# Output tiles and small copies on ScalarE, no identity turns ahead of a read, another order of the work, in a fused attention and FFN kernel

## The chip, the cores and the metric

The kernel runs on one core of a Trainium2 chip. Its engines have queues of their own, each worked off in order: TensorE (PE for its matmuls, PEld for its weight loads), VectorE (DVE), ScalarE (ACT), GpSimd (POOL) and SyncE (SP), which issues most of the DMAs. The metric is the time of one execution on the device in microseconds, the median of several runs.

## The reference

```python
# x (8, 8, 512, 64): B, H, S, D;  state (8, 8, 32, 64): B, H, Ns, D
scores = scale * x @ state^T;   a  = softmax(scores)   # over the 32 states
xread  = a @ state                                     # (B, H, 512, 64)
scores2 = scale * state @ x^T;  a2 = softmax(scores2)  # over the 512 tokens
sread  = a2 @ x                                        # (B, H, 32, 64)
x_in = concatenate([xread, sread], axis=2)             # 544 tokens of a batch
x_in = x_in.transpose(0, 2, 1, 3).reshape(8 * 544, 512)
h = x_in @ w_in                  # w_in (512, 2048)
g = h * clip(h + 3, 0, 6) / 6
out = g @ w_out                  # w_out (2048, 512); out (4352, 512)
```

All inputs and the output are float32.

## The kernel before

A float32 product is made of three matmuls: both factors are split into a high part, rounded to the matmul's format (fp32r), and a low part, the rest; hi x hi, hi x lo and lo x hi add up in one bank (`product`, L1053). ScalarE makes the high parts (L402, and L524 for w_out), VectorE the low ones (L403, L526). Weights come as 16-bit halves that are put together on chip (L492 on ScalarE, L497 on VectorE).

The FFN runs in two sweeps over the hidden dimension. A sweep has a unit for each batch b (512 tokens, four tiles of 128), and a small unit for all state tokens; a unit has eight steps, one for each 128 hidden columns. In a step TensorE forms a hidden tile in a `ps_h` bank (L1053; in the opening's first steps one plain float32 matmul for each part, L1274); ScalarE takes relu(h + 3) into `g` (L1295), VectorE min(., 6) times h (L1298), both split g into `g_hi` and `g_lo`, and TensorE multiplies it with the step's rows of w_out into four accumulators `acc0` to `acc3`, one for each tile of tokens (L1053, plain ones L1355). The attention is folded into that: the scores' softmax weights are multiplied with state times w_in (`wp_hi`, `wp_lo`, made from L630) instead of with the state first. At a unit's end in the first sweep the accumulators, times 1/6, go to an output tile `ot` in `put_out`: tiles with an even number by ScalarE (L1380), the others by VectorE (L1383), and from there to the partial result. The second sweep (from about 320 us) goes over the other half of the hidden columns and works with sums of quarters (L1165).

The second softmax is made beside the first sweep. For b = 0 its weights are turned by TensorE (L940) and copied by ScalarE (L944); `tokens_read_alone` then lets TensorE read the tokens (L1008), for b = 0 behind eleven identity turns (L1034). The result, divided and turned, goes to `sread_t` through `put` (L985, eight copies of 128x128). Identity turns of another kind (L1660) stand in the opening wherever the plan leaves TensorE a gap.

No loop sets the order of the instructions. Every operation is put on a list by `plan.add` with an engine, an estimated cost, what it reads and writes, and `Plan.order` schedules it: each engine takes, of the operations that can start within 0.3 us of the earliest, the one with the lowest number in RANKS (L24 to L133, a number for each operation). `issue` emits the instructions in that order, and each engine's queue keeps it. So the table decides what stands behind what on an engine; buffers and banks are given out in that order too.

The names in the rows: `raw`, `early` are staging tiles of weights or of x, `tops` high halves of weights, `tmp` tiles of 128x512, `st_raw` the state, `a0hi` and `a0lo` copies of the split weights of b = 0 that are stored in memory for the second sweep (L1424). L617 loads 64 KB of x for the transposes L720, which make the x that the scores L630 of the next batch need; four tiles of 128x512 are one batch, four loads make one, eight stand in one buffer `raw`.

Of the kernel before, what the change touches and what calls it, by code (L numbers as in the profile page):

```python
# [279 lines left out]
def tile_state_attention_then_hardswish_ffn(  # L280
# [8 lines left out]
    nc = tc.nc  # L289
    B, H, S, D = x.shape  # L290
# [693 lines left out]
    def put(c, ps, cols):  # L984
        V(0.28, URGENT, lambda: nc.vector.tensor_copy(  # L985
            sread_t.rearrange("p q (n b) -> p q n b", b=B)[..., c],
            bank(ps)[:, cols].rearrange("p (q n) -> p q n", n=NS)), [ps], [("sread", c)],
            [scores_at[0]])
# [702 lines left out]
```

## Time and profile before

| what | value |
|---|---|
| median of 3 runs | 638.37 us (637.26 to 639.91) |
| the profiled execution | 639.32 us, its span 637.5 us |
| TensorE matmuls | 630.1 us busy, 4388 instructions |
| VectorE | 520.4 us (82%), 946 instructions |
| ScalarE | 343.9 us (54%), 611 instructions |
| granted TensorE clock | 1.00 |

The span is what the profiler sees between the first and the last instruction; 1.82 us of the execution lie around it. Matmuls are pipelined, so that the durations of their records overlap: in a run of products one of 128x512 starts every 0.23 us, while its record says 0.39. An idle time in square brackets behind a row is the time that the engine stood idle before it, and what ended that.

### The profile page before, as it was taken

The numbers are of one execution on the slowest core, as the hardware profiler recorded it, in microseconds if no ns is written. First come the engines' busy times: TensorE is split into PE (matmuls) and PEld (weight loads), VectorE is DVE, ScalarE is ACT, GpSimd is POOL, SyncE is SP. The second block draws the span as 40 slices with busy tenths as digits, with TensorE's granted clock in tenths as the row PEclk, the third lists the DMA queues.
The fourth block names the chain that finished last, engine by engine and source line by source line (L and its number), as shares of the span: only waits on it lengthen the run. The fifth ranks groups of instructions, "written<-read, shape, count | busy, mean of one in ns | idle before, by whom it ended". The sixth has DMA issues, their size and how long they took to land.

```text
span 637.5 us, 11454 instructions
## 1 busy us (share of the span) xinstructions
PE 630.1 (99%) x4388; PEld 528.3 (83%) x4388; DVE 520.4 (82%) x946; ACT 343.9 (54%) x611; POOL 18.4 (3%) x22
## 2 busy tenths in 40 slices
PE   8999999999999999999999999999999999999997
PEld 7467778777777778778888888899999999999996
DVE  5999998988988797885568738999979899988773
ACT  4865565545555554454446657665455455554431
POOL 0000000000000000000000000000000000001010
PEclk9999999999999999999999999999999999999999
DMA  8987995967687695540312868324626225522244
GB/s 293 268 224 122 260 175 142 213 153 207 110 208 176 149 219 117 141 99 9 93 67 87 293 209 228 110 38 97 133 34 166 34 34 125 107 34 34 34 67 99
DMA packets 168261, 86.18 MB, mean 135 GB/s; under 512 B 128528, under 2 KB 152976, under 8 KB 168080
## 3 DMA queue, kind: packets, MB, share of 16 engines
q1 hardware_dynamic: 164240, 77.47, 46.9%
q0 software_dynamic: 3824, 7.87, 8.6%
q8 instruction: 34, 0.56, 0.4%
q14 instruction: 19, 0.16, 0.1%
q10 hardware_dynamic: 144, 0.13, 0.1%
HBM read 50.84 MB, written 34.60 MB: 134 GB/s over the span
## 4 chain that ended last, share of the span: by engine, by line
PE 92%; SPq 2%; DMA 2%; DVE 1%; ACT 1%; issue 0%
PE acc L1053 31%; PE acc L1165 24%; PE ps_h L1053 23%; PE ps_s L1053 7%; PE ps_s L630 2%; SPq L617 2%; DMA st_raw<-in_state_dram 2%; PE ps_s L1491 1%; PE ps_h L1008 1%; PE acc L1491 1%; PE ps_h L630 1%; PE acc L1355 1%; DMA raw<-in_x_dram 0%; PE acc L730 0%; PE ps_s L794 0%
## 5 line engine op out<-in xcount | busy, mean ns | idle before, releaser
L1053 PE MATMUL acc<-w_out_hi,g_hi 128*128 128x512 f32 x296 | 118.2, 399 | 0.3 <-ACT g_hi L402 0.3
L1053 PE MATMUL acc<-w_out_lo,g_hi 128*128 128x512 f32 x296 | 115.5, 390 | 0.0
L1053 PE MATMUL acc<-w_out_hi,g_lo 128*128 128x512 f32 x296 | 115.4, 390 | 0.0
L1165 PE MATMUL acc<-w_out_hi,tmp 128*128 128x256 f32 x360 | 87.9, 283 | 0.0
L1295 ACT ACTIVATE g<-ps_h,three 128x512 f32<-128x512 f32 (+1 forms) x80 | 51.2, 646 | 57.9 <-PE ps_h L1053 52.3
L1298 DVE SCALAR_TENSOR_TENSOR g<-g,ps_h 128x512 f32<-128x512 f32 (+1 forms) x80 | 50.1, 629 | 27.6 <-ACT g L1295 27.0
L1053 PEld LDWEIGHTS acc<-w_out_hi,g_hi 128*128 128x128 f32 x296 | 55.6, 188 | 19.4 <-issue 7.0
L1165 PE MATMUL acc<-w_out_hi,g_lo 128*128 128x256 f32 x240 | 68.0, 283 | 0.0
L1165 PE MATMUL acc<-w_out_lo,g_hi 128*128 128x256 f32 x240 | 67.9, 283 | 0.0
L1165 PE MATMUL acc<-w_out_hi,g_hi 128*128 128x256 f32 x240 | 67.9, 283 | 0.0
L1053 PE MATMUL ps_h<-aT_hi,wp_hi 128*128 128x512 f32 (+1 forms) x188 | 67.6, 360 | 0.0
L1165 PEld LDWEIGHTS acc<-w_out_hi,tmp 128*128 128x128 f32 x360 | 66.4, 192 | 0.3
L1053 PE MATMUL ps_h<-aT_lo,wp_hi 128*128 128x512 f32 (+1 forms) x188 | 66.5, 354 | 0.0
L1053 PE MATMUL ps_h<-aT_hi,wp_lo 128*128 128x512 f32 (+1 forms) x188 | 66.4, 353 | 0.0
L1053 PEld LDWEIGHTS acc<-w_out_hi,g_lo 128*128 128x128 f32 x296 | 55.6, 188 | 12.3 <-DVE g_lo L403 0.4
L1053 PEld LDWEIGHTS acc<-w_out_lo,g_hi 128*128 128x128 f32 x296 | 55.6, 188 | 10.7 <-issue 0.3
L402 ACT CAST g_hi<-G 128x512 fp32r<-128x512 f32 (+1 forms) x64 | 38.2, 606 | 46.8 <-PE acc L1165 38.7
L402 ACT CAST g_hi<-g 128x512 fp32r<-128x512 f32 (+1 forms) x74 | 42.7, 585 | 27.3 <-DVE g L1298 16.6
L403 DVE TENSOR_TENSOR g_lo<-g,g_hi 128x512 fp32r<-128x512 f32 (+1 forms) x74 | 46.8, 643 | 8.7 <-ACT g_hi L402 6.6
L1165 PE MATMUL acc<-w_out_lo,tmp 128*128 128x256 f32 x180 | 50.9, 283 | 0.0
L403 DVE TENSOR_TENSOR g_lo<-G,g_hi 128x512 fp32r<-128x512 f32 (+1 forms) x64 | 42.2, 669 | 6.1 <-ACT g_hi L402 5.5
L1165 PEld LDWEIGHTS acc<-w_out_hi,g_hi 128*128 128x128 f32 x240 | 46.0, 192 | 0.7
(179 smaller groups left out, 1277.5 us busy)
## 6 DMA issues: line engine op xcount, KB each, us to landing
out_dram<-ot SPq DMA_DIRECT2D x8, 1024.0 KB, 5.3
W<-G SPq DMA_DIRECT2D x16, 512.0 KB, 4.1
out_dram<-ot POOLq DMA_DIRECT2D x15, 512.0 KB, 6.0
raw<-in_x_dram SPq DMA_DIRECT2D x112, 64.0 KB, 2.9
xb<-in_x_dram SPq DMA_DIRECT2D x28, 256.0 KB, 4.7
raw<-in_moe_w_out_dram SPq DMA_DIRECT2D x11, 511.8 KB, 5.1
wp_lo<-W SPq DMA_DIRECT2D x40, 128.0 KB, 2.8
raw<-in_moe_w_in_dram SPq DMA_DIRECT2D x8, 511.0 KB, 5.5
```

The source lines that it names most:

```text
L402: first = S_(cost, rank, lambda: nc.scalar.copy(hi(), src()), reads, [writes[0]], after)
L403: V(cost, rank, lambda: nc.vector.tensor_tensor(lo(), src(), hi().bitcast(F32), op=ALU.subtract), [*reads, writes[0]], [writes[1]])
L617: nc.sync.dma_start(t[rows, i].rearrange("t (a c) -> t a c", c=NS), x[b, 4 * g + 2 * i + u, :, k * NS : (k + 1) * NS].rearrange("(a t) c - ...
L630: nc.tensor.matmul(out[u][cols, :], made["stT", b][rows, cols], moving(q)[rows], start=True, stop=True,)
L1008: nc.tensor.matmul(bank(pr)[cols, u * D : (u + 1) * D], e2T(b, u)[:, j * P + q * NS : j * P + (q + 1) * NS], x_tile(b, True)[:, NG * q + u ...
L1053: nc.tensor.matmul(ps, l, r, start=start and k == 0, stop=stop and k == n - 1)
L1165: nc.tensor.matmul(out, left(a, l), right(b, r), start=p == 0 and z == 0 and y == 0, stop=p == FPS // 2 - 1 and y == 2, skip_group_check=True)
L1295: in_turn["g", n] = S_(cost + 0.05, rank, lambda: nc.scalar.activation(g(), bank(ps)[:, :width], AF.Relu, bias=three, scale=-1.0 if turned ...
L1298: V(cost, rank, lambda: nc.vector.scalar_tensor_tensor(g(), g(), 6.0, bank(ps)[:, :width], op0=ALU.min, op1=ALU.mult), [ps], [g_key])
L1355: nc.tensor.matmul(bank(acc), made["g_hi", n][:, js], plain_out[f][1](), start=opens, stop=closes)
L1491: nc.tensor.matmul(bank(banks[q // 2][u])[:, q % 2 * W : (q % 2 + 1) * W], st[l]()[rows, q], wp(r)[rows, q], start=y == 0, stop=y == 2, sk ...
```

## The change

Four things: `put` copies on ScalarE instead of VectorE; the eleven identity turns of `tokens_read_alone` are gone (and the operation's estimated cost goes from + 0.2 to + 0.25); in `put_out` all four output tiles of a unit of the first sweep (b < B) go to ScalarE; and RANKS has other numbers. The lines behind L1034 are numbered two lower in the new kernel (L1295 is L1293, L1298 is L1296, L1380 is L1378).

```diff
 RANKS = [int(k) for k in """
-2 0 8 3 33 1 18 4 38 20 28 11 21 37 40 25 31 53 58 29 36 39 43 57
+2 0 7 3 27 1 11 4 31 13 24 10 14 30 33 23 26 43 47 25 28 32 34 46
...
     def put(c, ps, cols):
-        V(0.28, URGENT, lambda: nc.vector.tensor_copy(
+        S_(0.28, URGENT, lambda: nc.scalar.copy(
             sread_t.rearrange("p q (n b) -> p q n b", b=B)[..., c],
...
         def run():
-            for _ in range(0 if b else 11):
-                nc.tensor.transpose(bank(writes[0])[:, place(2)], ident, ident)
             turn_last()
             read()
-        T(cost + 0.2, rank, run, reads, writes, after)
+        T(cost + 0.25, rank, run, reads, writes, after)
...
             acc = acc_key(k, j)
-            if j % 2 == 0:
+            if j % 2 == 0 or b < B:
                 S_(0.62, rank, lambda j=j, acc=acc: nc.scalar.mul(ot()[:, j, :], bank(acc), 1.0 / 6.0),
```

The opening up to about 21 us keeps its order on all engines, and TensorE's order from about 320 us on is the old one. Between them it differs on every queue. Three places:

First ScalarE's queue at the start of the hidden tiles, about 21 to 29 us, before (`ps_s_243` and `ps_s_244` are the scores of the states, `ps_h_314` and `ps_h_332` the first two hidden tiles, `ps_s_352` state times w_in):

```order
L524 CAST w_out_hi0_224<-raw_132 128x512
L402 CAST aT_hi_323<-w_in2_200 128x512 x2
L906 ACTIVATE tmp_337,r2_338<-ps_s_244,nm2_299 128x512
L1295 ACTIVATE g_345<-ps_h_314,three_89 128x512
L906 ACTIVATE tmp_347,r2_338<-ps_s_243,nm2_295 128x512
L1295 ACTIVATE g_350<-ps_h_332,three_89 128x512
L492 CAST tops_91<-early3_182 128x512
L402 CAST wp_hi_369<-ps_s_352 128x256
```

and now:

```order
L524 CAST w_out_hi0_224<-raw_132 128x512
L906 ACTIVATE tmp_322,r2_323<-ps_s_244,nm2_299 128x512
L906 ACTIVATE tmp_328,r2_323<-ps_s_243,nm2_295 128x512
L492 CAST tops_91<-raw_141 128x512
L492 CAST tops_91<-early3_182 128x512
L1293 ACTIVATE g_356<-ps_h_315,three_89 128x512
```

The two casts to `aT_hi` left this place, both L906 stand together, and the first hidden tile's relu (L1293) has two L492 ahead of it. On VectorE the next step of that tile, L1296, has two L497 ahead of it now:

```order
L909 TENSOR_SCALAR r2_323<-r2_323 128x2
L911 RECIPROCAL r2_323<-r2_323 128x2
L497 SCALAR_TENSOR_TENSOR raw_141<-raw_141,tops_91 128x512
L497 SCALAR_TENSOR_TENSOR early3_182<-early3_182,tops_91 128x512
L1296 SCALAR_TENSOR_TENSOR g_356<-g_356,ps_h_315 128x512
```

Before, L1298 of the first tile stood ahead of L909 and of both L497.

Then SyncE's queue, issued between about 31 and 55 us, before (`raw_335` and `raw_407` hold the x of b = 1, `raw_544` and `raw_546` that of b = 2, `raw_498` weights):

```order
L479 DMA early3_395<-in_moe_w_out_dram 128x2x2047
L617 DMA raw_335<-in_x_dram 32x16x32
L617 DMA raw_407<-in_x_dram 32x16x32 x7
L617 DMA raw_335<-in_x_dram 32x16x32
L617 DMA raw_407<-in_x_dram 32x16x32
L1424 DMA a0lo_482<-aT_lo_330 128x1024
L1424 DMA a0hi_494<-aT_hi_323 128x1024
L479 DMA raw_498<-in_moe_w_in_dram 128x4x511
L553 DMA st_raw_502<-in_state_dram 32x4x32 x4
```

and now:

```order
L617 DMA raw_338<-in_x_dram 32x16x32 x3
L1422 DMA a0hi_400<-aT_hi_365 128x1024
L617 DMA raw_338<-in_x_dram 32x16x32
L617 DMA raw_436<-in_x_dram 32x16x32 x3
L617 DMA raw_338<-in_x_dram 32x16x32
L617 DMA raw_436<-in_x_dram 32x16x32 x5
L1422 DMA a0lo_499<-aT_lo_371 128x1024
L553 DMA st_raw_502<-in_state_dram 32x4x32 x4
L617 DMA raw_533<-in_x_dram 32x16x32 x2
L479 DMA raw_545<-in_moe_w_in_dram 128x4x511
L617 DMA raw_533<-in_x_dram 32x16x32 x2
L617 DMA raw_570<-in_x_dram 32x16x32 x8
```

The store a0hi stands ahead of ten of the loads of x now, and the load of weights behind the states and two loads of x. Of the sixteen loads for b = 2 four more of `raw_533` follow; the eight of the buffer that is transposed first (`raw_570`) end as the twelfth, where those of `raw_546` ended as the fifteenth.

Last TensorE's queue at the first states' read, about 56 to 62 us, before (each product is three rows):

```order
L1053 MATMUL ps_h<-aT_hi,wp_lo 128x512
L1053 MATMUL acc_372<-w_out_hi_457,g_hi 128x512
L1053 MATMUL acc_372<-w_out_lo_468,g_hi 128x512
L1053 MATMUL acc_372<-w_out_hi_457,g_lo 128x512
L1034 MATMUL ps_s<-ident 128x128 x11
L1008 MATMUL ps_s<-xb,tmp 32x64 x32
L1053 MATMUL acc_366<-w_out_hi_457,g_hi 128x512
```

and now:

```order
L1051 MATMUL ps_h<-aT_hi,wp_lo 128x512
L1051 MATMUL acc_379<-w_out_hi_443,g_hi 128x512
L1051 MATMUL acc_379<-w_out_lo_452,g_hi 128x512
L1051 MATMUL acc_379<-w_out_hi_443,g_lo 128x512
L1051 MATMUL acc_367<-w_out_hi_443,g_hi 128x512
L1051 MATMUL acc_367<-w_out_lo_452,g_hi 128x512
L1051 MATMUL acc_367<-w_out_hi_443,g_lo 128x512
L1051 MATMUL acc_398<-w_out_hi_443,g_hi 128x512
L1051 MATMUL acc_398<-w_out_lo_452,g_hi 128x512
L1051 MATMUL acc_398<-w_out_hi_443,g_lo 128x512
L1008 MATMUL ps_s<-xb,tmp 32x64 x32
L1051 MATMUL acc_379<-w_out_hi_443,g_hi 128x512
```

The turns are gone, and three products instead of one stand between the hidden tile and the read. The product behind the read uses the g of that hidden tile in both. The turning of the weights (L940), which stood ahead of that hidden tile, is done some 15 products earlier now.

## Rows read from the trace of the kernel before

**Rows 1.** The page: busy time of each engine, share of the span, instructions
```profile
PE 630.1 (99%) x4388; PEld 528.3 (83%) x4388; DVE 520.4 (82%) x946; ACT 343.9 (54%) x611; POOL 18.4 (3%) x22
```

**Rows 2.** TensorE's waits in the whole run: total us, times, longest us
```profile
PE ps_h L1660 <- POOL ident masks.py:199: 1.6, 1, 1.6
PE ps_s L707 <- DMA st_raw<-in_state_dram: 0.6, 1, 0.6
...
PE acc L1053 <- ACT g_hi L402: 0.3, 1, 0.3
...
PE ps_s L630 <- ACT tmp L906: 0.2, 1, 0.2
```

**Rows 3.** Timeline of the first states' read: start us, us, engine, line, operation
```profile
55.96 1.08 ACT L944 COPY tmp<-ps_s 128x512 f32<-128x512 f32 x2 [0.67 <-PE ps_s L940]
...
57.08 1.31 DVE L720 STREAM_TRANSPOSE tmp<-raw 128x512 f32<-128x512 f32 x2 [1.03 <-DMA raw<-in_x_dram]
...
57.80 0.69 ACT L1295 ACTIVATE g<-ps_h,three 128x512 f32<-128x512 f32 x1 [0.77 <-PE ps_h L1053]
...
58.29 1.36 PE L1034 MATMUL ps_s<-ident 128*128 128x128 f32 x11
...
58.99 0.69 DVE L751 TENSOR_TENSOR tmp<-tmp,m 128x512 f32<-128x512 f32 x1
...
59.58 1.10 PE L1008 MATMUL ps_s<-xb,tmp 128*32 128x64 f32 x64
59.60 0.68 DVE L1298 SCALAR_TENSOR_TENSOR g<-g,ps_h 128x512 f32<-128x512 f32 x1
...
60.32 1.14 ACT L402 CAST g_hi<-g 128x512 fp32r<-128x512 f32 x2
...
60.99 0.50 PE L1053 MATMUL acc<-w_out_hi,g_hi 128*128 128x512 f32 x1 [0.31 <-ACT g_hi L402]
...
61.72 0.50 PE L1053 MATMUL acc<-w_out_hi,g_lo 128*128 128x512 f32 x1
```

**Rows 4.** Timeline of the opening, the first hidden tiles
```profile
22.11 1.16 ACT L402 CAST aT_hi<-w_in 128x512 fp32r<-128x512 f32 x2
...
23.15 0.71 ACT L906 ACTIVATE tmp<-ps_s,nm 128x512 f32<-128x512 f32 x1
...
24.83 0.68 DVE L1298 SCALAR_TENSOR_TENSOR g<-g,ps_h 128x512 f32<-128x512 f32 x1
...
25.84 4.77 PE L1355 MATMUL acc<-raw,g 128*128 128x512 f32 x10
...
28.67 1.45 ACT L492 CAST tops<-early 128x512 f16<-128x512 bf16 x2
```

**Rows 5.** Timeline of the scores of b = 1 and the transposes ahead
```profile
42.58 1.30 DVE L720 STREAM_TRANSPOSE tmp<-raw 128x512 f32<-128x512 f32 x2 [0.32 <-DMA raw<-in_x_dram]
...
44.45 1.09 PE L630 MATMUL ps_s<-tmp,stT 64*32 64x512 f32 x16
```

**Rows 6.** Busy us in a stretch, PE PEld DVE ACT POOL, clock, DMA share, GB/s
```profile
40.00:45.00 5.00, 5.00 (x36) 3.58 (x35) 4.33 (x8) 2.81 (x4) 0.00 (x0) 1.00 0.82 240
```

**Rows 7.** Groups by line and form: total us, mean ns, idle before, releaser
```profile
L1383 DVE TENSOR_SCALAR ot<-acc 128x512 f32<-128x512 f32 x17 | 11.7, 688 | 9.9 <-PE acc L1053 9.8
...
L1380 ACT ACTIVATE ot<-acc 128x512 f32<-128x512 f32 x17 | 10.1, 597 | 8.7 <-PE acc L1053 8.6
...
L985 DVE COPY sread_t<-ps_h 128x128 f32<-128x128 f32 x6 | 2.4, 399 | 0.0
```

**Rows 8.** Busy us in two stretches of 20 us, the opening and the sweep
```profile
0.00:20.00 20.00, 17.12 (x146) 14.02 (x147) 12.20 (x26) 9.95 (x19) 0.95 (x7) 1.00 0.89 295
...
100.00:120.00 20.00, 20.00 (x160) 15.77 (x159) 16.20 (x30) 11.29 (x21) 0.00 (x0) 1.00 0.75 210
```

**Rows 9.** Timeline of TensorE in the opening: one operation, two paces
```profile
4.13 1.12 PE L730 MATMUL acc<-ident,xb 128*128 128x128 f32 x4
...
11.13 0.61 PE L730 MATMUL acc<-ident,xb 128*128 128x128 f32 x4
```

126 rows, old and new, of the table RANKS are left out of this document.

## The prediction

> **What bounds the kernel now.** I read the share of each engine first: TensorE is busy 99% of the span [rows 1], and in the windows its granted clock stands at 1.00, the 2.4 GHz level, in the opening as in the sweep [rows 8]. So an edit can move the time only where it removes TensorE work, or where TensorE waits before or after the edit. Then the list of TensorE's waits [rows 2]: six in the whole run, the longest 1.6 us, the shortest 0.2, and all of them before 62 us. In the first sweep behind that, up to 320 us, it idles nowhere: a window there has it busy 20.00 of 20.00 us [rows 8]. Then the timeline of the two places the change touches before that point: the opening from 22 to 26 us [rows 4] and the first states' read at 57 to 62 us [rows 3]. The reader is to see two things there. At 58.29 eleven identity turns (L1034) run ahead of the read; the turned weights that the read needs were copied at 55.96 to 57.04, so the turns cover no wait of the read itself. And right behind the read TensorE stands twice, at 60.99 for g_hi and at 61.72 for g_lo: the read (64 matmuls from 59.58, which take 0.83 us when the next follows at their pace) would have let the product start at 60.41 and its third matmul would have followed the second by 0.23 us at 61.45, so the holes are 0.58 and 0.27, 0.85 us in all. The list of waits has only 0.3 of it [rows 2], since it counts idle time from the modelled end of the matmul before.
>
> Why is g late? VectorE's queue answers: L1298, which makes g, stands behind two L720 transposes of the next unit's x (which waited 1.03 us for their transfer), then L749 and L751; it starts at 59.60 although ScalarE's half was done at 58.49 [rows 3].
>
> **The change part by part.** The sum is made against the profiled execution's own 639.32 us (span 637.5, 1.82 around it). The median of the three runs shown is 638.37, 0.95 less; that offset is taken off at the end.
>
> 1. The turns. They hold TensorE from 58.29 to 59.58: 1.29 us go. Minus 1.29, if nothing else is late at the read. Its inputs (57.04) are not.
>
> 2. What is late next: the stall behind the read. With the old order the turns' removal would gain nothing, since the product waits for g whatever stands ahead. The new order puts three products, nine matmuls, between the ps_h product and the read where one stood, so the distance from ps_h to g's first use is nine matmuls of 0.228 us plus the read, 2.9 us, nearly the same as before with the turns (0.69 + 1.29 + 0.83 = 2.8). But on VectorE L1296 (the old L1298) now comes ahead of L751, and the x tile that its L720s wait for is no longer loaded last: its eight loads end twelfth of the sixteen instead of fifteenth. Walked: L720s from 56.3 to 57.6, one L403, L1296 done 58.9, g_hi 59.5, g_lo 60.2; TensorE wants them at 60.2 and 60.7. The stall goes: minus 0.85. If the transfer is only as early as it was (57.08), g_hi comes at 60.3 and g_lo at 61.0: then about 0.35 of the 0.85 stays.
>
> 3. The opening. On ScalarE the two casts to aT_hi go behind, and both exponentials L906 move up to their place at 22.11; then two tops casts L492 come ahead of L1293, the relu of the first hidden tile, and on VectorE their two L497 come ahead of L1296. Walk: two L906 at 0.68 start to start end the pair by 23.5; two L492 (1.45 for a pair) by 24.9; the second L497 waits for that and ends at about 25.6; L1296 needs another 0.68 and g is there at 26.2 to 26.4. Before, g was done at 25.51 and the first plain product L1355 started at 25.84, straight behind the sixteen L630 matmuls [rows 4]. Those L630 no longer wait for L906 (0.2 in [rows 2]), but that only makes TensorE stand earlier. So the first plain product starts near 26.4: plus 0.6. Bounds: 0, if L1296 is not held by the casts, up to 1.0, if each step takes its full duration. The second hidden tile and the moved aT casts come in time by the same walk, each with some 0.3 us to spare.
>
> 4. The loads. On SyncE the store a0hi moves ahead of ten of the loads of x that b=1's scores need. Their last transpose L720 ended at 43.88 and the scores started at 44.45 [rows 5], a cover of 0.57. A store of 524 KB at the 240 GB/s of that stretch [rows 6] takes 2.2 us of all engines; the loads land about 2 us later, their transposes end near 45.9, and TensorE, itself 0.6 late and with another product order, is there at about 45.4. Plus 0.5. Bounds: 0 (the queue's issue sets the pace, not the transfer) and 2.0 (the whole store shows). I take the lower half since the loads behind the store are issued one by one and partly overlap it. A load of w_in also goes behind four of the state and two of x; what waits for it on ScalarE and VectorE has 1.3 us to spare in my walk at the wp_lo split: 0, and 1 as its upper bound, inside the range.
>
> 5. The output tiles and copies. Sixteen output tiles move from VectorE (688 ns each) to ScalarE (597), eight 128x128 copies from VectorE (399) to ScalarE [rows 7]; the copy on ScalarE is not shown, and lies below the 597 of four times its elements. ScalarE gets at most 16 x 0.597 + 8 x 0.597 = 14.3 us over a sweep of some 260 us, 1.1 in 20; it is busy 11.29 of 20 us there, VectorE 16.20 [rows 8]. Both evictions wait for TensorE before they run (8.7 and 9.9 us), not the other way. So 0, covered by TensorE itself, which runs the next unit's first ps_h products while the banks are emptied; my walk of the new queue leaves 1.7 us between the last eviction and the first use of its bank. If that cover were gone it would be the third rival.
>
> The row for this job favours ScalarE: 597 ns against 688. The Trainium skill, page "ScalarE: Activation LUTs", section "Rules for kernel authors", says the opposite for multiplications (use VectorE, which it calls up to about three times faster, in bf16); this case's float32 tiles from PSUM don't bear that out. By the rule the move would be a loss wherever ScalarE is the engine waited for, which is the third rival; by the rows it is none.
>
> Sum: -1.29 - 0.85 + 0.60 + 0.50 = -1.04, so 638.28 for an execution like the profiled one, and 637.3 against the median.
>
> 6. The rest of the sweep is written in another order on all queues, with the same instructions. There is nothing to win there (no waits) and a loss only by a new wait. From 320 us on TensorE's order is the old one. Counted 0.
>
> **The rivals.**
>
> A. The transfer keeps the stage. If the x tile lands no earlier in relation to the read, the turns' 1.29 us turn into waiting on g, and the stage ends when it did. The opening's 1.1 us vanish in the same wait. For it: L720 waited 1.03 us for its transfer [rows 3], and no edit makes a transfer faster. Against: the tile's loads end three places earlier. Result: no change, 638.4.
>
> B. The opening costs nothing (bounds 0 in steps 3 and 4): 638.37 - 1.29 - 0.85 = 636.2. For it: ScalarE and VectorE have some slack right behind. Against: the walk.
>
> C. Slower: four output tiles in ScalarE's one queue. At each of the eight unit ends four evictions of 0.6 us now come one behind the other, where two and two ran beside each other; ScalarE, in order, holds the next unit's relu L1293 behind an eviction whose accumulator is not closed (such tiles waited 8.7 us over 17 of them [rows 7]). From the point where that wait plus two more tiles (1.2 us) exceeds the slack of 1.7 us, TensorE waits for a bank or a g. Price: one eviction more than the slack covers, 0.6 us, at each of eight ends, +4.8: 642.1. Against it: ScalarE idles nearly half of the time [rows 8].
>
> D. The clock. TensorE's opening matmuls run at half the later pace: four of L730 take 1.12 us at 4.13 and 0.61 at 11.13 [rows 9], although the granted clock of that window reads 1.00 [rows 8]. If a new hole of half a microsecond at 26 or 45 us brought that pace back for as long as these two rows lie apart, 7 us, half of it would be lost, 3.5: 640.8. Against it: the holes of 0.58 and 0.27 behind the read were followed by matmuls at the pace of before [rows 3].
>
> The Trainium skill, page "TensorE: Matmul & The Clock Gate", Part 1, calls the throttled clock the default that only activity lifts; by that rule idle turns like the ones removed are worth keeping. Here the products on both sides of them keep TensorE at work, and the trace shows no lower level at that place.
>
> **How the numbers follow.** Chances: the forecast with its steps, 636.5 to 638.2, 0.55; A, 0.18; B, 0.13; C or another new wait of this kind in the rewritten sweep, 0.12 (a third of it under 4.3 us); D, 0.02. A single measurement of this kernel tells 0.5%, 3.2 us, from no change. Faster by more than that (under 635.2) needs B and a sweep gain that the waits don't show: 0.05. Slower (over 641.6): the dearer part of C: 0.08. Same: 0.87. The range that holds the time 8 times in 10 runs from 635.5, B's end with a little of run-to-run spread (the runs shown spread over 2.65), to 639.9, A with the same.
>
> **What would show it.** In the new profile: no L1034; the read right behind the third product at 58.5 to 59.5 us; no wait of TensorE on g_hi or g_lo behind it (step 2; a wait of 0.3 to 1.5 there is A); a wait of 0.4 to 0.7 on g ahead of the first plain product near 26 us (step 3); a wait of 0 to 1 on L720's tmp near 45 us (step 4); no wait on an output tile or a relu behind one at the unit ends between 80 and 320 us (step 5). The time of 320 us to the end should be the old one. The forecast is wrong if TensorE's waits over 0.3 us after 62 us add up to more than 1, or if the read starts no earlier than 59.58.

## The result and the profile after

The changed kernel takes 647.71 us (median of 6 runs, 646.68 to 651.32), against 639.48 us of the kernel before in the same comparison: a ratio of the means (648.29 and 639.01) of 1.0145, 95% interval 1.0114 to 1.0177. The numbers of the kernel before are those of five of its six runs, 637.26 to 640.01; the sixth took 1037.76 us and is left out. The changed kernel is slower, 10.4 us over the forecast of 637.3 and outside the range of 635.5 to 639.9.

The profiled execution is the longest of the six: 651.32 us, its span 649.5. Section 1 of its page, which answers to [rows 1]:

```profile
PE 635.6 (98%) x4377; PEld 531.2 (82%) x4377; DVE 509.1 (78%) x922; ACT 354.7 (55%) x635; POOL 18.3 (3%) x22
```

VectorE has 24 instructions and 11.3 us of work less and ScalarE 24 and 10.8 us more: the sixteen tiles and the eight copies. TensorE executes 11 instructions less, yet its share fell from 99 to 98%. The list of TensorE's waits, beside [rows 2]:

```profile
PE ps_h L1051 <- DVE g L1296: 5.5, 3, 4.2
...
PE acc L1353 <- DVE g L1296: 1.1, 1, 1.1
...
PE acc L1051 <- DVE g_lo L403: 0.5, 1, 0.5
PE ps_h L1051 <- DVE aT_lo L403: 0.4, 1, 0.4
```

The first row is new, and one wait in it is 4.2 us long. The windows of the same kernel say where; the columns are those of [rows 8]:

```profile
100.00:120.00 20.00, 15.81 (x65) 12.73 (x64) 11.22 (x21) 8.21 (x14) 0.00 (x0) 0.92 0.52 137
...
114.00:116.00 2.00, 0.00 (x0) 0.00 (x0) 0.57 (x1) 0.00 (x0) 0.00 (x0) 1.00 0.53 110
116.00:118.00 2.00, 0.64 (x2) 0.54 (x3) 1.31 (x3) 0.60 (x2) 0.00 (x0) 0.75 0.75 246
118.00:120.00 2.00, 2.00 (x6) 1.61 (x5) 1.80 (x3) 1.76 (x4) 0.00 (x0) 0.50 0.80 263
120.00:122.00 2.00, 2.00 (x16) 1.40 (x22) 1.53 (x3) 1.68 (x4) 0.00 (x0) 0.90 0.06 9
```

The stretch from 100 to 120 us, in which TensorE was busy 20.00 us before, has it at 15.81. Nothing runs on it, on ScalarE or (almost) on VectorE from 114 to 116 us, and behind the hole the granted clock is 0.50 for two microseconds: only 6 matmuls in 2 us there. The timeline of that place:

```profile
107.29 1.30 DVE L720 STREAM_TRANSPOSE tmp<-raw 128x512 f32<-128x512 f32 x2
...
108.61 0.39 SPq L979 DMA_DIRECT2D raw<-e  x1
...
109.05 4.31 SPq L617 DMA_DIRECT2D raw<-in_x_dram  x4
...
115.43 1.30 DVE L720 STREAM_TRANSPOSE tmp<-raw 128x512 f32<-128x512 f32 x2 [6.85 <-DMA raw<-in_x_dram]
116.66 0.65 DVE L1296 SCALAR_TENSOR_TENSOR g<-g,ps_h 128x512 f32<-128x512 f32 x1
...
117.36 0.80 PE L1051 MATMUL ps_h<-aT_hi,wp_hi 128*128 128x512 f32 x1 [4.18 <-DVE g L1296]
```

Read it from the bottom. TensorE waits for a `ps_h` bank, which comes free when L1296 has read it into g; L1296 stands in VectorE's queue behind two transposes L720; these wait 6.85 us for their x; the four loads of that x stand on SyncE behind L979; and L979 is issued at 108.61, right when the transposes of 107.29 end. L979 loads the turned weights of the second softmax of b = 2 into a buffer `raw`, of which there are three, given out in the order of the program, and the one that it got held the x which those transposes read. So a load waits for a buffer, and four loads that need nothing wait behind it. The list of SyncE's waits has the price (two of its rows):

```profile
SPq L479 <- DVE tmp L720: 18.3, 8, 7.5
...
SPq L979 <- DVE tmp L720: 5.6, 1, 5.6
```

In the kernel before, the buffer was just as late, but all sixteen loads of that x stood ahead of L979. Nobody stood behind it who was in a hurry. Its timeline, and the row of L979 in its list of SyncE's waits:

```profile
106.30 0.70 DVE L720 STREAM_TRANSPOSE tmp<-raw 128x512 f32<-128x512 f32 x1
107.03 0.37 SPq L979 DMA_DIRECT2D raw<-e  x1
```

```profile
SPq L979 <- DVE tmp L720: 6.7, 2, 5.6
```

In the changed kernel the row of L979 itself says 0.39 us and no wait. The Trainium skill, page "Perfetto Trace Analysis", section "DMA Instruction — HWDGE (DVE, Sync)", says why such a row is silent: the profiled row of a DMA issue begins when the semaphores are satisfied, the wait ahead of it isn't in it. This trace agrees (0.39 us in the row, 5.6 in the list of SyncE's waits).

The longest of the eight waits in the row of L479 above, 7.5 us, is the same kind of wait at a second place, 30 us earlier:

```profile
76.73 0.37 SPq L479 DMA_DIRECT2D raw<-in_moe_w_in_dram  x1
...
80.96 0.79 ACT L490 ACTIVATE tops<-raw 128x512 f16<-128x512 bf16 x1 [3.69 <-DMA raw<-in_moe_w_in_dram]
81.78 0.69 DVE L497 SCALAR_TENSOR_TENSOR w_in<-raw,tops 128x512 uint32<-128x512 uint32 x1 [3.72 <-ACT tops L490]
...
89.58 0.50 PE L1051 MATMUL ps_h<-aT_hi,wp_hi 128*128 128x512 f32 x1 [1.14 <-DVE g L1296]
...
92.88 0.50 PE L1051 MATMUL acc<-w_out_hi,g_lo 128*128 128x512 f32 x1 [0.51 <-DVE g_lo L403]
```

A load of w_in waits for another `raw` buffer whose x is transposed until 76.7, and is issued at 76.73. VectorE and ScalarE, in order, stand 3.7 us for it, and TensorE pays later, at 89.58 and 92.88.

A sum over all holes, each as the time by which the end of a matmul came later than its usual pace: 5.96 at 117 (4.76 for the hole and 1.2 for the slow matmuls behind it), 1.42 at 89.6, 0.79 at 92.9, 0.44 at 83, 0.66 at 70.0, 0.45 at 73.0, together 9.72. Minus 1.29 for the turns, minus 0.65 for the old stall (the prediction had 0.85; see step 2 below), plus 0.41 in the opening: +8.19. Measured from the first hidden tile's first matmul (20.82 before, 24.77 after) to the end of the last one (633.50 and 645.52): 612.68 and 620.75, so +8.07. The sum accounts for it but for 0.12 us. The other 3.95 us of the profiled execution lie ahead of that tile and seem to belong to that run (last section): it is the longest of the six, and the medians are 8.23 apart, near the 8.07.

### The profile page after: what moved, and what is told of

It is laid out like the page before. It is cut to its first block, busy times and chain, and to the rows that moved or that the text cites. A ratio compares the mean times of both kernels' runs of the same rounds, so it can differ in the third digit from the quotient of the medians.

```text
span 649.5 us, 11413 instructions
## 1 busy us (share of the span) xinstructions
PE 635.6 (98%) x4377; PEld 531.2 (82%) x4377; DVE 509.1 (78%) x922; ACT 354.7 (55%) x635; POOL 18.3 (3%) x22
## 4 chain that ended last, share of the span: by engine, by line
PE 81%; SPq 1%; DMA 0%; DVE 0%; issue 0%; DVEq 0%
PE acc L1051 26%; PE acc L1163 23%; PE ps_h L1051 20%; PE ps_s L1051 7%; PE ps_s L630 2%; PE ps_s L1489 1%; PE acc L1489 1%; PE ps_h L1008 1%; PE ps_h L630 1%; SPq L617 1%; DMA raw<-in_x_dram 0%; DVE tmp L720 0%; PE ps_s L1008 0%; DVE ot L1235 0%; DVE g L1296 0%
## 5 line engine op out<-in xcount | busy, mean ns | idle before, releaser
L1293 ACT ACTIVATE g<-ps_h,three 128x512 f32<-128x512 f32 (+1 forms) x80 | 51.2, 646 | 46.0 <-PE ps_h L1051 42.3
L1296 DVE SCALAR_TENSOR_TENSOR g<-g,ps_h 128x512 f32<-128x512 f32 (+1 forms) x80 | 49.6, 628 | 30.4 <-ACT g L1293 29.8
L1051 PEld LDWEIGHTS acc<-w_out_hi,g_hi 128*128 128x128 f32 x296 | 55.8, 188 | 18.0 <-issue 3.4
L1051 PEld LDWEIGHTS acc<-w_out_lo,g_hi 128*128 128x128 f32 x296 | 55.8, 189 | 10.4
L1051 PEld LDWEIGHTS ps_h<-aT_hi,wp_hi 128*128 128x128 f32 x188 | 35.8, 190 | 13.9 <-DVE g L1296 7.4
```

The lines of the kernel that those rows point to most:

```text
L1051: nc.tensor.matmul(ps, l, r, start=start and k == 0, stop=stop and k == n - 1)
L1293: in_turn["g", n] = S_(cost + 0.05, rank, lambda: nc.scalar.activation(g(), bank(ps)[:, :width], AF.Relu, bias=three, scale=-1.0 if turned ...
L1296: V(cost, rank, lambda: nc.vector.scalar_tensor_tensor(g(), g(), 6.0, bank(ps)[:, :width], op0=ALU.min, op1=ALU.mult), [ps], [g_key])
```

## The experiments

The column "rest" is the stretch just named, in the profiled execution of each. It leaves out the first 20 us, whose length changes from run to run.

| kernel | median us (runs) | ratio to before, 95% | rest, us |
|---|---|---|---|
| before | 638.38 to 639.48 (a median for each comparison) | 1 | 612.68 |
| changed | 647.71 (6) | 1.0145 [1.0114, 1.0177] | 620.75 |
| old_table | 658.09 (4) | 1.0299 [1.0281, 1.0317] | |
| table_only | 662.33 (5) | 1.0371 [1.0352, 1.0389] | |
| x_home | 641.35 (6) | 1.0041 [1.0027, 1.0054] | 615.09 |
| l979_late | 641.59 (11) | 1.004 [1.0028, 1.0052] | 615.25 |
| x_two | 638.68 (12) | 1.0004 [0.9991, 1.0017] | 612.62 |
| turns_back | 638.92 (12) | 0.9998 [0.998, 1.0017] | 612.92 |
| tiles_back | 640.13 (12) | 1.0021 [1.0004, 1.0037] | 613.89 |
| best | 637.99 (12) | 0.9988 [0.9969, 1.0006] | 612.43 |
| no_turns | 639.11 (12) | 1.0013 [0.9998, 1.0028] | 612.13 |

**The table and the edits apart.** old_table is the changed code with the numbers of before, table_only the code of before with the new numbers.

```diff
 RANKS = [int(k) for k in """
-2 0 7 3 27 1 11 4 31 13 24 10 14 30 33 23 26 43 47 25 28 32 34 46
+2 0 8 3 33 1 18 4 38 20 28 11 21 37 40 25 31 53 58 29 36 39 43 57
```

> The changed kernel with the old table RANKS: the three code edits stay (copies and output tiles on ScalarE, no turns), and the plan orders them by the old numbers. Theory 1 (the new table's order on SyncE makes the loss): the code edits cost nothing to speak of, 637 to 641 us, ratio to before 0.995 to 1.003. Theory 2 (rival C of the prediction, four output tiles in ScalarE's queue): 644 us or more, with TensorE waits at unit ends.

> The kernel before with the new table RANKS alone; turns, VectorE copies and VectorE output tiles as before. Theory 1 (the table): 645 to 651 us, ratio 1.010 to 1.018, again with a SyncE issue that waits for VectorE's L720 while loads of x stand behind it. Theory 2 (the evictions on ScalarE): within 2 us of before.

Both are far slower than either kernel, 2.99 and 3.71%. table_only lies outside both of its theories; old_table lies in the range of its second one, but not for that reason: of TensorE's waits there only 0.7 us is on an output tile, and at the longest, 2.2 us at 222, ScalarE itself stands waiting for VectorE's g. TensorE's longest waits in table_only:

```profile
PE ps_h L1053 <- DVE sread_t L985: 7.9, 4, 2.8
PE ps_h L1053 <- DVE g L1298: 3.3, 3, 2.8
```

and the longest in old_table:

```profile
PE acc L1051 <- ACT g_hi L402: 4.4, 3, 2.2
```

These are other waits than those of the changed kernel, so the two runs don't split its loss into a part of the table and a part of the code. They show that here neither half of the change does well without the other: the new numbers lose time on the old list of operations, and the old numbers on the new list. All later experiments but no_turns keep the order of the changed kernel and change little in it.

**A place of its own for L979.** x_home gives L979's tile a place that lies unused at that time; all queues keep their order.

```diff
-        made_of = lambda key: get(key, lambda: stage.tile([P, NG, S], F32, name="raw"))
+        made_of = lambda key: get(key, lambda: cpool.tile(
+            [P, NG, S], F32, name="w_in3", tag="w_in3") if key[1] == ("e2T", 2) else
+            stage.tile([P, NG, S], F32, name="raw"))
```

> The changed kernel, same order on every queue; only the tile that the DMA L979 of b = 2 writes lies in a place of its own (that of w_in3, unused then) and no longer in one of the three raw buffers, so that this DMA need not wait for the L720 that empties one. Theory 1: SyncE issues the four loads of x behind it near 103 us, and TensorE's wait of 4.2 us near 113 and the slow matmuls behind it (1.2 us) go: 641 to 643 us, 4.5 to 6.5 less than the changed kernel. Theory 2 (the late g there comes from ScalarE's evictions or VectorE's own order): 646 to 648, no gain.

641.35 us: 6.4 of the 8 us are back with one buffer moved. L979 (L981 here) and the four loads behind it are issued without waiting, so the loads themselves needed nothing. The hole at 117 and the slow matmuls are gone, those of the second place remain (line numbers are two higher here):

```profile
84.64 0.50 PE L1053 MATMUL ps_h<-aT_hi,wp_hi 128*128 128x512 f32 x1 [1.17 <-DVE g L1298]
...
98.24 0.43 SPq L981 DMA_DIRECT2D w_in<-e  x1
98.72 2.85 SPq L617 DMA_DIRECT2D raw<-in_x_dram  x4
```

**L979 behind the loads.** l979_late leaves the buffers as they are and moves one instruction on one queue: L979 goes behind the four loads of x. The number is that of the operation in the list.

```diff
-            for n in self.order(RANKS):
+            row = self.order(RANKS)
+            for n, ahead in [(432, 416)]:
+                row.remove(n)
+                row.insert(row.index(ahead), n)
+            for n in row:
```

> The changed kernel with one instruction moved: on SyncE the DMA L979 of b = 2 goes behind the last four loads of x instead of ahead of them; every other queue has the same order, and the buffers are shared as before. Theory 1 (L979 holds the loads behind it): as x_home, 640.5 to 643 us, TensorE's wait of 4.2 us gone. Theory 2 (three raw buffers are too few for this order, wherever L979 stands): 646 or more, the wait turns up at the read L1008 or at another load.

641.59 us, the same as x_home within the intervals. So it takes both, the taken buffer and the loads behind it; to undo either is enough.

**The second place.** x_two is x_home with the tile of the load at 76.73 in such an unused place too.

```diff
-                return get(place, lambda: stage.tile([P, 512, 2], U32, name="raw")).unsqueeze(1)
+                return get(place, lambda: cpool.tile(
+                    [P, 512, 2], U32, name="w_in3", tag="w_in3") if place[1] == ("in", 10) else
+                    stage.tile([P, 512, 2], U32, name="raw")).unsqueeze(1)
```

> As x_home, and the staging tile of the first load of w_in of that unit (issued at 76.7 in the changed kernel, behind an L720) lies there too. Theory 1: ScalarE's wait of 3.7 us for that load goes, and with it TensorE's small waits between 83 and 93 us (together about 2.5): 638.5 to 641 us. If those waits come from VectorE's order and not from the load: as x_home.

638.68 us: no difference from the kernel before. The waits at 83, 89 and 93 us are gone; two buffers account for the whole loss. What is left of TensorE's waits on VectorE (lines four higher):

```profile
PE acc L1357 <- DVE g L1300: 1.2, 1, 1.2
...
PE ps_h L1055 <- DVE aT_lo L403: 0.5, 1, 0.5
```

With the accident out of the way, x_two serves as the base on which the parts of the change can be weighed.

**The turns.** turns_back puts the eleven turns back into x_two, all else in the same order.

```diff
         def run():
+            for _ in range(0 if b else 11):
+                nc.tensor.transpose(bank(writes[0])[:, place(2)], ident, ident)
             turn_last()
```

> x_two (638.68 us) with the eleven identity turns put back ahead of the first states' read, same order everywhere. Step 1 of the prediction (the turns hold TensorE and cover nothing): 1.0 to 1.4 us more, 639.7 to 640.1. Rival A (what they take is waited for anyway): 638.4 to 639.0.

638.92 us, the same as x_two, as rival A had it; in the rest +0.30, not +1.29. The rows of turns_back:

```profile
57.99 1.36 PE L1038 MATMUL ps_s<-ident 128*128 128x128 f32 x11
...
59.29 1.10 PE L1012 MATMUL ps_s<-xb,tmp 128*32 128x64 f32 x64
...
65.19 0.69 DVE L403 TENSOR_TENSOR aT_lo<-tmp,aT_hi 128x512 fp32r<-128x512 f32 x1
```

and of x_two:

```profile
58.44 1.10 PE L1012 MATMUL ps_s<-xb,tmp 128*32 128x64 f32 x64
...
65.19 0.68 DVE L403 TENSOR_TENSOR aT_lo<-tmp,aT_hi 128x512 fp32r<-128x512 f32 x1
...
65.92 0.50 PE L1055 MATMUL ps_h<-aT_lo,ot 128*128 128x512 f32 x1 [0.49 <-DVE aT_lo L403]
```

VectorE makes aT_lo at 65.19 in both. Counted from the first hidden tile (19.98 and 20.21) the read starts 1.08 us later with the turns. TensorE arrives earlier without the turns and waits there; with them it finds aT_lo done, and the list has no such wait.

**The turns alone.** no_turns is the kernel before without its turns (the same three lines taken out), all else in its old order.

> The kernel before with the 11 identity turns ahead of the first states' read left out and nothing else changed: same places of all other instructions on every queue. The turns end 1.29 us of TensorE's time ahead of the read, and the read's own stall of 0.85 us stands behind them. Theory A (the time that the turns free is waited for again some microseconds later, on VectorE's transposed halves, as the kernel with the turns put back showed): 638.3 to 639.2, within 0.1% of the kernel before, with a longer wait on aT_lo or g between 65 and 76 us. Rival (the time is kept): 637.3 to 637.8 against 638.9, a ratio near 0.998. Third: the turns' place was what let the read's transfer land, and the stall grows by as much: the same time as theory A, but with the wait at the read itself (over 1.5 us at about 62 us) and none later.

639.11 us, no gain that can be told. In its trace the wait behind the read, 0.31 in [rows 3], has become 1.10. It stands at the read, where the third theory put it, though smaller than that theory said, and not later as in theory A:

```profile
57.71 1.10 PE L1008 MATMUL ps_s<-xb,tmp 128*32 128x64 f32 x64
...
59.91 0.50 PE L1051 MATMUL acc<-w_out_hi,g_hi 128*128 128x512 f32 x1 [1.10 <-ACT g_hi L402]
```

Of the 1.29 us 0.8 went into that wait at once; the rest of the profiled run is 0.55 shorter, but twelve timed runs don't show it.

**The tiles.** tiles_back is x_two with the odd output tiles and the eight copies on VectorE again, at the same places in the program.

```diff
-        S_(0.28, URGENT, lambda: nc.scalar.copy(
+        S_(0.28, URGENT, lambda: nc.vector.tensor_copy(
...
-                S_(0.62, rank, lambda j=j, acc=acc: nc.scalar.mul(ot()[:, j, :], bank(acc), 1.0 / 6.0),
+                S_(0.62, rank, lambda j=j, acc=acc: (nc.vector.tensor_scalar_mul if j % 2 else nc.scalar.mul)(ot()[:, j, :], bank(acc), 1.0 / 6.0),
```

> x_two with the sixteen odd output tiles of the first sweep and the eight copies to sread_t on VectorE again, at the same place of the order, so that TensorE's, SyncE's and GpSimd's queues are the same. Step 5 of the prediction (it costs and gives nothing): 638.0 to 639.4. Rival C (four evictions in one queue cost): 1.5 us or more less than x_two, 637.2 or lower. If VectorE was the one with too little room: 1.5 or more above it.

640.13 us, 1.45 over x_two, and 1.27 in the rest. The two were timed in different comparisons, with the kernel before at 638.92 and 638.90 us, and their intervals against it overlap a little; the size is better read from the rest. The rows show where most of it arises:

```profile
63.73 0.65 DVE L1382 TENSOR_SCALAR ot<-acc 128x512 f32<-128x512 f32 x1
...
65.50 0.68 DVE L1382 TENSOR_SCALAR ot<-acc 128x512 f32<-128x512 f32 x1
66.10 0.68 DVE L403 TENSOR_TENSOR aT_lo<-tmp,aT_hi 128x512 fp32r<-128x512 f32 x1
...
66.83 0.50 PE L1055 MATMUL ps_h<-aT_lo,ot 128*128 128x512 f32 x1 [1.65 <-DVE aT_lo L403]
```

Two output tiles on VectorE stand ahead of the aT_lo for which TensorE waits, and the wait grows from 0.49 to 1.65. Counted from the first hidden tile (20.26 and 20.21) that product starts 0.86 us later than in x_two; the remaining 0.4 come later, most of it in two small steps near 159 and 222 us. So this part of the change is worth over a microsecond, in this order of the work. The eight copies went back together with the tiles and were not tried alone.

**The best version.** best is x_two with three instructions moved in the emitted row, by the same lines as in l979_late with the list (118, 60), (119, 61), (206, 291): the first hidden tile's relu ahead of the two L492, its second step ahead of the two L497, and aT_lo ahead of ot.

> x_two with three instructions moved: ScalarE's L1293 and VectorE's L1296 of the first hidden tile go ahead of the L492 and L497 that the new order puts first (step 3 of the prediction: 0.4 us in the traces), and VectorE's second aT_lo of b = 1 ahead of the ot that it follows (TensorE waited 0.4 to 0.6 us for it near 66 us). If both waits are ended by these queues: 0.7 to 1.2 us less than x_two, 637.4 to 638.0, 0.1 to 0.25% below the kernel before. If something else ends them: 638.5 or more.

637.99 us, 0.12% under the kernel before with an interval that includes no change. It beats the changed kernel; against the one before it can't be told. In the rest it is only 0.19 us shorter than x_two, where 0.7 to 1.2 had been expected. The first plain product no longer waits, but the second g does:

```profile
24.17 2.96 PE L1361 MATMUL acc<-raw,g 128*128 128x512 f32 x6
...
27.84 2.52 PE L1361 MATMUL acc<-raw,g 128*128 128x512 f32 x5 [0.71 <-DVE g L1304]
```

From 20 to 30 us of that run VectorE is busy 9.74 and ScalarE 10.00 us, so a step moved ahead makes another late.

## Why the prediction was wrong

**Step 6 failed.** "The rest of the sweep is written in another order ... a loss only by a new wait. ... Counted 0." There were new waits of 9.72 us in it, 8.61 of them at 83 to 120 us and due to two buffers (x_home, l979_late, x_two); the other 1.11 are told of below. "No waits" in the trace of before was read as "no risk"; it says only that the old order kept TensorE supplied, and nothing of how much slack the other queues had, which the forecast did not look at behind 62 us except at the unit ends. The order of the new program, known beforehand, had the place in it: L979 ahead of four loads of x, where before it stood behind all of them. What was missing was to ask, for every load that moved on SyncE, which buffer it gets and when that comes free.

**Steps 1 and 2** hold at their place: no turns, the read right behind the third product, and no wait on g behind it. The rows of the changed kernel, beside [rows 3]:

```profile
61.62 0.67 DVE L1296 SCALAR_TENSOR_TENSOR g<-g,ps_h 128x512 f32<-128x512 f32 x1
...
62.60 1.10 PE L1008 MATMUL ps_s<-xb,tmp 128*32 128x64 f32 x64
...
63.63 0.50 PE L1051 MATMUL acc<-w_out_hi,g_hi 128*128 128x512 f32 x1
```

Less the 3.95 us by which this run is late, the read stands at 58.65, in the forecast's 58.5 to 59.5. The stall that goes was smaller than step 2 had it. It took 0.83 us from the read's start to the next product; here, and at all seven other reads of the kernel before, it is 1.03, as in these rows of the kernel before:

```profile
112.13 1.10 PE L1008 MATMUL ps_h<-xb,raw 128*32 128x64 f32 x64
113.16 0.50 PE L1053 MATMUL acc<-w_out_hi,g_hi 128*128 128x512 f32 x1
```

So the first of the two holes is 0.38, not 0.58, and the stall 0.65, not 0.85. And of the 1.94 us (1.29 and 0.65) 1.11 are given back at 70.0 and 73.0, on aT_lo and g (0.66 and 0.45): VectorE, busy 9.86 of the 10 us from 60 to 70, sets the pace there as soon as TensorE runs ahead. On the base without the two buffer waits the turns come to 0.30 us of TensorE's time and to no difference that can be timed (turns_back), where step 1 had 1.29. Rival A had this: the gain turns into a wait. It named the wait right behind the read, where no_turns shows it; in the new order it stands seven and ten microseconds later.

**Step 3** had the right sign and place, 0.41 for 0.60. The rows beside [rows 4]:

```profile
28.86 0.69 DVE L497 SCALAR_TENSOR_TENSOR early<-early,tops 128x512 uint32<-128x512 uint32 x1
29.46 0.68 DVE L1296 SCALAR_TENSOR_TENSOR g<-g,ps_h 128x512 f32<-128x512 f32 x1
30.20 2.97 PE L1353 MATMUL acc<-raw,g 128*128 128x512 f32 x6 [1.14 <-DVE g L1296]
```

The wait is 1.14, over the forecast's 0.4 to 0.7, since TensorE came earlier; from the first hidden matmul to this product it is 5.43 us against 5.02.

**Step 4** cost nothing for 0.50: the last L720 ahead of the scores ended at 48.32 and L630 started at 49.04 without a wait. The lower bound held.

**Step 5** was counted 0 and is worth 1.3 to 1.45 us (tiles_back). The step looked at whether TensorE waits for the tiles, which it does not, and at ScalarE's load. It did not ask what stands behind the tiles in VectorE's queue.

**Rival C** named the kind, "another new wait of this kind in the rewritten sweep", at 0.12, but put its place and price on ScalarE's evictions. These still wait for TensorE and not the other way; the group beside [rows 7]:

```profile
L1378 ACT ACTIVATE ot<-acc 128x512 f32<-128x512 f32 x33 | 19.6, 601 | 12.2 <-PE acc L1051 12.0
```

**Rival D** did occur, as a part of the big hole and not at the places looked at: 1.2 us (last section).

Open: why the plan took this order. It counts a buffer as free by its own giving out of the buffers, and in the built program L979 got another one than the plan had in mind; that was read from the program, not tried, and no row here shows the plan's own choice.

## What to carry to other kernels

When a whole program is written in another order, a trace without waits is no evidence that the new order has none. Go down the queue that issues the loads, and ask for each load that moved which buffer it takes, who reads that buffer last, and who stands behind the load; a DMA row of 0.4 us can hold the next four for 5.6. Time that one edit frees is kept only as far as the next engine has slack: here VectorE took back most of it within some eight microseconds.

## What the runs showed of the hardware

After 4.18 us without a matmul the granted clock fell: 0.75 in the slice of 116 to 118 us, 0.50 (the 1.2 GHz level) from 118 to 120, 0.90 from 120 to 122, then 1.00. The products of 128x512 started 0.43 us apart instead of 0.23 for six of them, 1.2 us in all. The holes of 1.1 to 1.7 us behind 20 us in the other kernels of the table, old_table and table_only aside, have matmuls of the usual pace behind them. How long a hole is does not settle it alone: in table_only the clock stayed at 1.00 behind one of 2.81 us (product at 86.14), and read 0.53 from 98 to 100 us behind one of 2.14 (product at 96.73). The Trainium skill, page "TensorE: Matmul & The Clock Gate", Part 1, has two levels of the clock gate, an idle array falling to the lower; the rows agree, with 0.75 and 0.90 as slices that hold both.

The opening has two paces as well, and when it changes from the slow to the fast one differs from run to run of nearly the same program: the four L730 of 0.6 us instead of 1.1 appear at 5.89 us in l979_late, at 11.13 in the kernel before, and not by 13.4 in the profiled execution of the changed one:

```profile
12.52 1.06 PE L730 MATMUL acc<-ident,xb 128*128 128x128 f32 x4
13.38 3.52 PE L794 MATMUL ps_s<-sread_t,w_in 128*128 128x64 f32 x16
```

L794 took 1.94 us in the kernel before at that place. This is the 3.95 us of that execution, and most of the spread between runs may be it. The column of the granted clock reads 1.00 there all the same, as in [rows 8]; the prediction took that for the 2.4 GHz level in the opening too. The trace keeps no clock record ahead of the change of pace: its first one, to 1.00, lies at 5.7 us in l979_late, at 9.8 in the kernel before and at 21.4 in this execution. So the opening's pace is to be read from the rows.
